# Wider rows for wo and w1, w2's last part halved, and the residual loaded by small transfers, in a decode step of grouped-query attention beside a Mish layer

## The chip, the cores and the metric

The kernel runs on one core of a Trainium2 chip. The metric is device time in microseconds, the median of three runs; every array is float32 and the batch is 8 tokens with one position each.

## What is computed

The input x (8 x 512) is normalised once, and two branches are added to it.

```python
xn = _layernorm(x, axis=-1)
return x + _A_ref(xn, A_k_cache, A_v_cache, A_wq, A_wo) + _B_ref(xn, B_w1, B_b1, B_w2)
```

Branch A is attention: q = xn @ wq gives 32 heads of 128; 8 heads of keys and values, each shared by 4 query heads, hold 8192 cached positions; p = softmax(q k / sqrt(128)), o = p v, and o @ wo (4096 x 512). Branch B is h = xn @ w1 + b1 (512 x 1792), h * tanh(softplus(h)), and then @ w2 (1792 x 512).

## The kernel before

**Memory and units.** The cached keys and values are 512 MiB of the 535 MiB that are read, and everything is read once. The work is cut into 32 units: unit j = (m, b) is the token b = j % 8 with the pair m = j // 8 of key heads. A unit has one key block k(j) and one value block v(j), each 128 rows of 64 KiB, 8 MiB (load_unit, L119). All blocks live in one large tile kv: values at V_AT, keys alternately at two places K_AT that overlap by half, w1 at W1_AT (where the second key block will come), and at the end wo over the place of the values and w2 behind it.

**One unit** (loop at L441). scores(j) multiplies the key block in two halves (L279, 64 matmuls); between the halves SP issues the next key block k(j+1) (L450). softmax(j) takes the maximum and the exponential (L289 to L313). values(j-1) multiplies the value block before (L341, 64 matmuls), after which SP issues v(j) (L458) into the place that has just come free. key_weights(j+1) (L257) prepares the next keys' weights on VectorE. turn(j) (L315) turns the exponentials for values, and merge(j-1) (L356) puts unit j-1's output, divided by the softmax sum, into oT. Once per m, at b = 4, 5, 6 and 7, load_q, project, selections and spread prepare the queries of the next pair.

**What sets the order.** The order is the program's (`tc.manual_schedule()`): each engine takes its instructions in turn, and semaphores are put in by the framework. All large transfers are issued by SP, in one queue, and an instruction of SP that waits holds all that stand behind it. x and b1 alone are issued by ScalarE.

**Start.** SP issues wq's first part (L117), k(0) (L123), w1 (L434) and k(1). w1 waits until the small region of kv that holds x and its normalised copy xc has been read. From xc TensorE makes xn4 (L185, for the queries), xnT (L187, for w1), and from x the residual xres (L193, copied at L200). Then project and spread run (L218 to L251), and the units begin.

**mish** (L362) runs in unit 0: 32 matmuls of xnT with w1, some 15 instructions on VectorE, and at last aT (L404). Its scratch lies where w1 was, so that k(2) waits for aT.

**End** (L475 to L508). wo comes in four transfers of 2 MiB (L477), w2 in four parts (L486). outputs(m) (L409) multiplies oT with wo's part m, down (L421) multiplies aT with w2's parts into H, res = H + xres (L507), and out is stored (L508).

**How the weights lie.** wo[4m:4(m+1)] is read as `u p f -> p u f`, so a partition gets four rows of 4 KiB; w1 as `j p f -> p j f`, eight rows of 3.5 KiB; w2's parts are rows of 8 KiB, the last one of 4 KiB:

```python
parts = ((0, 2), (2, 4), (4, 6), (6, 7))
for lo, hi in parts:
    t = kv[:, W2_AT + lo * BW : W2_AT + hi * BW]
    nc.sync.dma_start(t, w2_rows[:, lo * BW : hi * BW])
```

Of the kernel before, what the change touches and what calls it, by code (L numbers as in the profile page):

```python
# [14 lines left out]
B = 8  # L15
# [34 lines left out]

W2R = 7
# [10 lines left out]
LOAD_Q, MAKE_Q, SPREAD_Q = 4, 5, 7  # L62


@with_exitstack
def kernel(
# [39 lines left out]
    xnT = const.tile([P, CC, B], F32, name="xnT")  # L106
    qr = const.tile([P, DI, H2 * B], F32, name="qr")
    xres = const.tile([P, P], F32, name="xres")
    oT = const.tile([P, NP, H2, B], F32, name="oT")
# [20 lines left out]
    low = kv[:B, W1_AT : W1_AT + 3 * D]  # L130
    x_sb, xc, sq = (low[:, i * D : (i + 1) * D] for i in range(3))
# [5 lines left out]
    w1_t = kv[:, W1_AT : W1_AT + 7168].rearrange("p (j f) -> p j f", j=2 * CC)  # L137
# [5 lines left out]
    nc.gpsimd.memset(pt8, 0.0)  # L143
    for t in (H, O, M):
        nc.vector.memset(t, 0.0)
# [7 lines left out]
    nc.vector.reduce_sum(bsel, ident.rearrange("p (g q) -> p q g", g=G), axis=AX.X)  # L153
    nc.vector.reduce_sum(hsel, ident.rearrange("p (c h) -> p h c", h=H2), axis=AX.X)
# [29 lines left out]
    for c in range(CC):  # L184
        nc.tensor.transpose(M[:, c * B : (c + 1) * B], xc[:, c::CC], ident[:B, :B])  # L185
    for c in range(CC):
        nc.tensor.transpose(  # L187
            M[:, 32 + c * B : 32 + (c + 1) * B], xc[:, c * P : (c + 1) * P], ident[:B, :B]
        )
    nc.vector.tensor_copy(xn4.rearrange("p c b -> p (c b)"), M[:, 0:32])  # L190
    nc.vector.tensor_copy(xnT.rearrange("p c b -> p (c b)"), M[:, 32:64])
    for g in range(G):
        nc.tensor.matmul(  # L193
            M[Q * g : Q * g + B, 256:384],
            ident[:B, :B],
            x_sb[:, g * P : (g + 1) * P],
            start=True,
            stop=True,
        )
    nc.vector.tensor_copy(xres, M[:, 256:384])  # L200
# [12 lines left out]
    def project():  # L213

        w = ws.rearrange("p (c f) -> p c f", c=CC)
        for d in range(2):
            for c in range(CC):
                nc.tensor.matmul(  # L218
                    H[Q * c : Q * c + B, :],
                    xn4[:, c, :],  # L220
                    w[:, c, d * 512 : (d + 1) * 512],
                    start=True,
                    stop=True,
                )
            qp = work.tile([P, 512], F32, name="e")
# [12 lines left out]
        return qT  # L238
# [50 lines left out]
    def softmax(j):  # L289
# [18 lines left out]
        e = E[j] = work.tile([P, 512], F32, name="e")  # L308
# [47 lines left out]
    def merge(j, os):  # L356
        m, b = divmod(j, B)
        nc.tensor.matmul(M[:, 168 : 168 + H2], os, hsel, start=True, stop=True)  # L358
        nc.vector.tensor_mul(oT[:, m, :, b], M[:, 168 : 168 + H2], RT.pop(j))


    def mish(w1_t, b1_sb, flat):  # L362
# [5 lines left out]
        for c in range(CC):  # L368
            for g in range(G):
                nc.tensor.matmul(  # L370
                    hp[Q * g : Q * g + B, :],
                    xnT[:, c, :],
                    w1_t[:, c * 2 + g // 2, g % 2 * FG : (g % 2 + 1) * FG],
                    start=False,
                    stop=(c == CC - 1),
                )
# [32 lines left out]
    def outputs(m, t):  # L409
        w = t.rearrange("p (u f) -> p u f", u=4)  # L410
        for d in range(2):
            for h in range(REP):
                nc.tensor.matmul(
                    A[Q * h : Q * h + B, :],
                    oT[:, m, d * REP + h, :],
                    w[:, d * 2 + h // 2, h % 2 * D : (h % 2 + 1) * D],
                    start=(m == 0 and d == 0),
                    stop=(m == NP - 1 and d == 1),
                )

    def down(lo, hi, w):  # L421
        for j in range(2 * lo, 2 * hi):
            for g in range(G):
                at = (j - 2 * lo) * D + g * P
# [7 lines left out]


    nc.sync.dma_start(w1_t, w1.rearrange("j p f -> p j f"))  # L434
# [6 lines left out]
    for j in range(UNITS):  # L441
# [34 lines left out]
    for m in range(NP):  # L476
        nc.sync.dma_start(  # L477
            w_o[m].rearrange("p (u f) -> p u f", u=4),
            wo[4 * m : 4 * (m + 1)].rearrange("u p f -> p u f"),
        )  # L480
    w2_rows = w2.rearrange("j p f -> (j p) f").rearrange("(q i) f -> q (i f)", i=W2R)
    w2_t = []
    parts = ((0, 2), (2, 4), (4, 6), (6, 7))
    for lo, hi in parts:
        t = kv[:, W2_AT + lo * BW : W2_AT + hi * BW]
        nc.sync.dma_start(t, w2_rows[:, lo * BW : hi * BW])  # L486
# [7 lines left out]
    a_sb = work.tile([P, 512], F32, name="e")  # L494
# [52 lines left out]
```

## Time and profile before

| what | value |
|---|---|
| median of 3 runs | 1312.41 us (1312.4 to 1312.55) |
| the profiled execution, its own time | 1312.45 us |
| its span, first to last instruction | 1310.7 us |
| HBM read | 561.01 MB |
| PE busy | 989.0 us, 75% |
| DVE busy | 515.1 us, 39% |
| instructions | 11149 |

The span is what the profile's views cover; the 1.75 us between it and the execution's own time lie around it. Times in the views are microseconds from the span's start. PE is TensorE's matmuls, PEld its weight loads, DVE VectorE, ACT ScalarE, POOL GpSimd, SPq the queue of SyncE (SP), which issues the transfers. GB/s and the DMA share in a window are counted at the ends of packets, so that a window shorter than some microseconds swings about its mean.

### The profile page before, as it was taken

How to read it: one execution, taken by the hardware profiler on the slowest of the kernel's cores; microseconds unless marked ns; L12 is line 12 of the kernel's file. 1: busy time of each engine (PE TensorE's matmuls, PEld its weight loads, DVE VectorE, ACT ScalarE, POOL GpSimd, SP SyncE). 2: the span in 40 equal slices, each digit the busy share in tenths (PEclk: the TensorE clock that was granted, in tenths of full speed). 3: DMA queues.
4: the chain of work that ended last, by engine and by line, in shares of the span. 5: the costliest groups of instructions: out<-in, count | busy, mean ns of one | idle time of the engine just before them, and what ended most of it. 6: DMA issues, size and time to landing. Idle time of an engine off the chain costs nothing.

```text
span 1310.7 us, 11149 instructions
## 1 busy us (share of the span) xinstructions
PE 989.0 (75%) x5040; PEld 340.5 (26%) x5040; DVE 515.1 (39%) x728; ACT 40.2 (3%) x88; POOL 2.2 (0%) x9
## 2 busy tenths in 40 slices
PE   5978867768877668777878777687686678677676
PEld 3222222222322222232322222232232222222222
DVE  3364334432444442335243344414444433344421
ACT  1000000000000000000000000000000000000000
POOL 0000000000000000000000000000000000000000
PEclk9988888898888888877888888888898898888898
DMA  9999999999999999999999999999999999999997
GB/s 393 451 422 439 427 436 430 432 439 429 441 429 433 431 437 425 447 415 447 423 439 433 427 441 423 443 425 439 429 435 431 435 431 437 432 435 421 441 414 322
DMA packets 13735, 561.79 MB, mean 429 GB/s; under 512 B 1260, under 2 KB 1392, under 8 KB 4600
## 3 DMA queue, kind: packets, MB, share of 16 engines
q1 hardware_dynamic: 13664, 561.06, 99.3%
q8 instruction: 39, 0.64, 0.2%
q10 hardware_dynamic: 24, 0.02, 0.0%
q14 instruction: 8, 0.07, 0.0%
HBM read 561.01 MB, written 0.07 MB: 428 GB/s over the span
## 4 chain that ended last, share of the span: by engine, by line
DMA 72%; PE 23%; DVE 2%; SPq 2%; issue 0%; ACT 0%; DVEq 0%
DMA kv<-in_v 71%; PE o L341 20%; SPq L486 1%; DMA kv<-in_w 1%; PE s L279 1%; DVE pt L329 1%; PE x L244 1%; PE h L370 0%; PE m L229 0%; PE h L218 0%; DVE kv L392 0%; DVE tr L323 0%; DVE wk L262 0%; DVE nm L291 0%; ACT L177 0%
## 5 line engine op out<-in xcount | busy, mean ns | idle before, releaser
L279 PE MATMUL s<-kv,wk 128*64 128x512 f32 x2048 | 504.4, 655 | 174.6 <-DMA kv<-in_kT 171.9
L341 PE MATMUL o<-kv,pt 128*32 128x512 f32 x2048 | 268.6, 684 | 54.9 <-DMA kv<-in_v 45.3
L279 PEld LDWEIGHTS s<-kv,wk 128*64 128x64 f32 x2048 | 155.6, 151 | 498.0 <-issue 320.6
L329 DVE TENSOR_REDUCE pt<-tr 64x512 f32<-64x2048 f32 x64 | 241.3, 3771 | 1.6
L291 DVE TENSOR_REDUCE nm<-s 128x1 f32<-128x512 f32 x32 | 22.1, 691 | 366.7 <-PE s L279 366.7
L318 PE MATMUL x<-e,perm 128*128 128x512 f32 x256 | 128.4, 648 | 2.0 <-ACT qr L251 2.0
L341 PEld LDWEIGHTS o<-kv,pt 128*32 128x32 f32 x2048 | 69.9, 123 | 227.1 <-issue 169.6
L349 DVE TENSOR_SCALAR os<-o,isel 128x128 f32<-128x128 f32 x32 | 11.2, 351 | 274.8 <-PE o L341 274.8
L323 DVE STREAM_TRANSPOSE tr<-x 128x512 f32<-128x512 f32 x128 | 78.7, 673 | 0.0
L262 DVE TENSOR_TENSOR wk<-qr,mask 128x512 f32<-128x512 f32 x64 | 63.0, 1026 | 19.7 <-ACT qr L251 19.7
L318 PEld LDWEIGHTS x<-e,perm 128*128 128x128 f32 x256 | 50.0, 206 | 76.2 <-issue 73.7
L310 ACT ACTIVATE e<-s,nmx 128x512 f32<-128x512 f32 x32 | 22.0, 687 | 1095.7 <-DVE nmx L307 1095.7
L351 DVE SCALAR_TENSOR_TENSOR os<-o,isel,os 128x128 f32<-128x128 f32 x96 | 33.7, 351 | 3.4
L292 PE MATMUL m<-ident,nm 128*1 128x128 f32 x32 | 8.7, 273 | 29.8 <-DVE nm L291 29.8
L303 PE MATMUL m<-ident,nx 1*128 1x1 f32 x32 | 7.0, 219 | 24.1 <-DVE nx L299 24.1
L244 PE MATMUL x<-qT,tr 128*128 128x64 f32 x128 | 19.3, 315 | 3.0 <-ACT qr L251 2.7
L321 DVE RECIPROCAL rt<-m 128x8 f32<-128x8 f32 x32 | 6.6, 207 | 36.1 <-PE m L319 36.1
L244 PEld LDWEIGHTS x<-qT,tr 128*128 128x128 f32 x128 | 18.1, 226 | 6.2 <-ACT qr L251 3.3
L358 PE MATMUL m<-hsel,os 128*128 128x8 f32 x64 | 12.4, 266 | 9.3 <-DVE rt L321 9.3
L312 DVE TENSOR_SCALAR lsel<-rsel,l 128x8 f32<-128x8 f32 x32 | 7.4, 231 | 30.1 <-ACT e L310 30.1
L292 PEld LDWEIGHTS m<-ident,nm 128*1 128x1 f32 x32 | 2.5, 79 | 58.0 <-DVE nm L291 58.0
L319 PEld LDWEIGHTS m<-lsel,ones 128*128 128x128 f32 x64 | 12.2, 190 | 15.4 <-issue 15.1
(88 smaller groups left out, 163.9 us busy)
## 6 DMA issues: line engine op xcount, KB each, us to landing
ws<-in_wq SPq DMA_DIRECT2D x4, 2048.0 KB, 34.3
kv<-in_wo SPq DMA_DIRECT2D x4, 2048.0 KB, 24.3
kv<-in_w SPq DMA_DIRECT2D x1, 3584.0 KB, 26.4
kv<-in_w SPq DMA_DIRECT2D x3, 1024.0 KB, 19.3
kv<-in_kT SPq DMA_DIRECT2D x32, 29.9
kv<-in_v SPq DMA_DIRECT2D x32, 30.2
kv<-in_w SPq DMA_DIRECT2D x1, 512.0 KB, 19.5
out<-os SPq DMA_DIRECT2D x1, 64.0 KB, 1.6
```

The costliest lines, as they stand in the source:

```text
L244: nc.tensor.matmul(X[:, half, k * 64 : (k + 1) * 64], wide[:, half * 8 + k], qT, start=True, stop=True,)
L262: nc.vector.tensor_mul(w[:, :, d], q[:, :, d].to_broadcast([P, DI, NH * G, REP]), mask[:, d * NH * G : (d + 1) * NH * G] .rearrange("p (o ...
L279: nc.tensor.matmul(S[64 * c : 64 * (c + 1), :], w[:, i].rearrange("p d k h -> p (d k h)"), kk[:, i, c, :], start=(part == 0 and n == 0), s ...
L291: nc.vector.tensor_reduce(nm, S, axis=AX.X, op=ALU.max, negate=True)
L310: nc.scalar.activation(e, S, AF.Exp, bias=nmx, accum_out=l)
L318: nc.tensor.matmul(X[:, g], perm[:, g], e, start=True, stop=True)
L323: nc.vector.transpose(tr.rearrange("p (l t) c -> p t l c", t=TL)[:, tl], X.rearrange("p g (t q l) -> p t l g q", t=TL, q=PP)[:, tl],)
L329: nc.vector.tensor_reduce(pt8[half, :, :, d * REP : (d + 1) * REP].rearrange("p c y h -> p y c h"), tr[half].rearrange("p y (g c h) -> p y ...
L341: nc.tensor.matmul(O[Q * q : Q * (q + 1), :], pt8[:, c, TL * l : TL * (l + 1), :].rearrange("p t h -> p (t h)"), vt[:, 512 * n : 512 * (n ...
L351: nc.vector.scalar_tensor_tensor(os, O[:, DH * i : DH * (i + 1)], isel[:, i : i + 1], os, op0=ALU.mult, op1=ALU.add)
L358: nc.tensor.matmul(M[:, 168 : 168 + H2], os, hsel, start=True, stop=True)
L486: nc.sync.dma_start(t, w2_rows[:, lo * BW : hi * BW])
```

## The change

Five edits go together.

1. wo's parts are read as 128 rows of 16 KiB (`(p f) -> p f`), so that a partition holds eight consecutive rows of the flat part. The outputs o are turned to match: after the last token of a pair, turn_o makes oX from oT with 16 small matmuls and one copy, and outputs uses oX.
2. w1 is read as 128 rows of 28 KiB. x is turned to match: xe is xc in another order (four copies on VectorE), 8 transposes, and two masked copies (hmask, one more reduction at the start) make x8 in place of xnT.
3. w2's last part of 1024 columns becomes two of 512.
4. The residual is no longer made from x on TensorE: GpSimd clears xres, and in unit 3, behind v(3), SP issues eight transfers that bring x's rows into it.
5. The tile "e" has one buffer in place of two, and project stands behind turn and merge in place of ahead of them.

```diff
+RESIDUAL = 3
+    x8 = const.tile([P, W1R, 2, B], F32, name="x8")
+    oX = const.tile([P, NP, CC, 2, B], F32, name="oX")
...
+    xe = kv[:B, W1_AT + 3 * D : W1_AT + 3 * D + W1R * P].rearrange("b (i s) -> b i s", i=W1R)
...
+    for c in range(CC):
+        nc.vector.tensor_copy(
+            xe.rearrange("b i (c h q) -> b c i h q", c=CC, h=2)[:, c],
+            xc[:, c * P : (c + 1) * P]
+            .rearrange("b (o q i) -> b i o q", o=1, i=W1R)
+            .to_broadcast([B, W1R, 2, P // CC // 2]),
+        )
+    for i in range(W1R):
+        nc.tensor.transpose(M[:, 32 + i * B : 32 + (i + 1) * B], xe[:, i], ident[:B, :B])
+    for h in range(2):
+        nc.vector.tensor_scalar(
+            x8[:, :, h],
+            M[:, 32 : 32 + W1R * B].rearrange("p (i b) -> p i b", i=W1R),
+            hmask[:, h : h + 1],
+            None,
+            op0=ALU.mult,
+        )
...
-        nc.vector.tensor_mul(oT[:, m, :, b], M[:, 168 : 168 + H2], RT.pop(j))
+        nc.vector.tensor_mul(oT[:, :, b], M[:, 168 : 168 + H2], RT.pop(j))
+        if b == B - 1:
+            turn_o(m)
+
+    def turn_o(m):
+
+        for i in range(CC):
+            for u in range(CC):
+                nc.tensor.matmul(
+                    M[Q * u : Q * (u + 1), 256 + 2 * B * i : 256 + 2 * B * (i + 1)],
+                    ident[:, i::CC],
+                    oT[:, 2 * u : 2 * u + 2].rearrange("p h b -> p (h b)"),
+                    start=True,
+                    stop=True,
+                )
+        nc.vector.tensor_copy(
+            oX[:, m].rearrange("p i h b -> p (i h b)"), M[:, 256 : 256 + 2 * CC * B]
+        )
...
+    def residual():
+
+        for g, n in enumerate((3, 6, 7, 4)):
+            for lo, hi in ((0, n), (n, B)):
+                nc.sync.dma_start(
+                    xres[Q * g + lo : Q * g + hi, :], x[lo:hi, g * P : (g + 1) * P]
+                )
...
-    nc.sync.dma_start(w1_t, w1.rearrange("j p f -> p j f"))
+    nc.sync.dma_start(w1_t, w1.rearrange("j p f -> (j p f)").rearrange("(p i f) -> p i f", p=P, i=W1R))
...
+        if j == RESIDUAL:
+            residual()
         if more and b == LOAD_Q:
             load_q(j // B + 1)
-        if more and b == MAKE_Q:
-            qT = project()
         turn(j, lsel)
         if j > 0:
             merge(j - 1, os)
+        if more and b == MAKE_Q:
+            qT = project()
...
-        nc.sync.dma_start(
-            w_o[m].rearrange("p (u f) -> p u f", u=4),
-            wo[4 * m : 4 * (m + 1)].rearrange("u p f -> p u f"),
-        )
+        rows = wo[4 * m : 4 * (m + 1)].rearrange("u p f -> (u p f)")
+        nc.sync.dma_start(w_o[m], rows.rearrange("(p f) -> p f", p=P))
...
-    parts = ((0, 2), (2, 4), (4, 6), (6, 7))
+    parts = ((0, 4), (4, 8), (8, 12), (12, 13), (13, 14))
```

In the last line the bounds count rows of 512 columns in place of 1024, and `down` follows them; `outputs` and `mish` take the new tiles with as many matmuls as before.

More of the change, by code (lines that the diff above doesn't have):

```diff
@@ L49 @@
 NJ = PL * HALF
+W1R = 8
 W2R = 7
@@ L143 @@
     nc.gpsimd.memset(pt8, 0.0)
+    nc.gpsimd.memset(xres, 0.0)
     for t in (H, O, M):
@@ L153 @@
     nc.vector.reduce_sum(bsel, ident.rearrange("p (g q) -> p q g", g=G), axis=AX.X)
+    nc.vector.reduce_sum(
+        hmask, ident.rearrange("p (c h q) -> p h c q", c=CC, h=2), axis=AX.XY
+    )
     nc.vector.reduce_sum(hsel, ident.rearrange("p (c h) -> p h c", h=H2), axis=AX.X)
@@ L185 @@
         nc.tensor.transpose(M[:, c * B : (c + 1) * B], xc[:, c::CC], ident[:B, :B])
+    nc.vector.tensor_copy(xn4.rearrange("p c b -> p (c b)"), M[:, 0:32])
     for c in range(CC):
-        nc.tensor.transpose(
-            M[:, 32 + c * B : 32 + (c + 1) * B], xc[:, c * P : (c + 1) * P], ident[:B, :B]
-        )
[L190 to L198, printed above, removed]
+        nc.vector.tensor_copy(
[3 more added lines that the diff above has]
+            .to_broadcast([B, W1R, 2, P // CC // 2]),
+        )
+    for i in range(W1R):
[7 more added lines that the diff above has]
+            op0=ALU.mult,
         )
-    nc.vector.tensor_copy(xres, M[:, 256:384])
     wide = tr.rearrange("p y c -> p (y c)").rearrange("p (i o) -> p i o", i=DI)
@@ L224, in project @@
                 )
-            qp = work.tile([P, 512], F32, name="e")
+            qp = work.tile([P, 512], F32, name="e", bufs=1)
             nc.scalar.copy(qp, H)
@@ L307, in softmax @@
         nc.vector.tensor_copy(nmx, M[:, 128:129])
-        e = E[j] = work.tile([P, 512], F32, name="e")
+        e = E[j] = work.tile([P, 512], F32, name="e", bufs=1)
         l = work.tile([P, 1], F32, name="l")
@@ L367, in mish @@
             )
-        for c in range(CC):
+        for i in range(W1R):
             for g in range(G):
@@ L409, in outputs @@
     def outputs(m, t):
[L410 to L418, printed above, removed]
-                )
+        for n in range(2 * CC):
+            i, h = divmod(n, 2)
+            q = n % G
+            nc.tensor.matmul(
+                A[Q * q : Q * q + B, :],
+                oX[:, m, i, h],
+                t[:, n * D : (n + 1) * D],
+                start=(m == 0 and n < G),
+                stop=(m == NP - 1 and n >= 2 * CC - G),
+            )
     def down(lo, hi, w):
-        for j in range(2 * lo, 2 * hi):
+        for j in range(lo, hi):
             for g in range(G):
-                at = (j - 2 * lo) * D + g * P
+                at = (j - lo) * D + g * P
                 nc.tensor.matmul(
@@ L493 @@
     outputs(NP - 1, w_o[NP - 1])
-    a_sb = work.tile([P, 512], F32, name="e")
+    a_sb = work.tile([P, 512], F32, name="e", bufs=1)
     nc.scalar.copy(a_sb, A)
```

17 lines of the change are left out of this document (8 added, 9 removed).

## The prediction

> **What bounds the kernel now.** I read the page first, then the chain of work that ended last, then windows of the transfers, then SP's own timeline.
>
> ```profile
> span 1310.7 us, 11149 instructions
> ...
> DMA  9999999999999999999999999999999999999997
> ...
> q1 hardware_dynamic: 13664, 561.06, 99.3%
> q8 instruction: 39, 0.64, 0.2%
> ...
> DMA 72%; PE 23%; DVE 2%; SPq 2%; issue 0%; ACT 0%; DVEq 0%
> ```
>
> The page's digits show transfer engines that are busy in every slice but the last, and SP's queue (q1) fills 99.3% of them. The chain says how: the value blocks.
>
> ```profile
> 161.44 31.53 DMA kv<-in_v
> 192.97 0.04 issue
> 193.02 8.81 PE o L341 x64
> 201.83 0.02 issue
> 201.85 29.82 DMA kv<-in_v
> ```
>
> ```profile
> 100.00:1262.00 1162.00, 883.23 (x4388) 299.54 (x4388) 455.19 (x624) 30.36 (x72) 0.00 (x0) 0.87 1.00 433
> ```
>
> The last number of a window is GB/s. v(3) is issued at 161.44, lands at 192.97, is used until 201.83, and v(4) takes its place. While TensorE uses a value block, the next key block is already in the queue, so the rate stays 433 GB/s. The time is the bytes by that rate plus both ends; compute that fits beside it costs nothing, and one microsecond of empty queue costs one.
>
> The engines don't finish together, though.
>
> ```profile
> 1300.00:1304.00 4.00, 2.35 (x64) 1.43 (x60) 0.00 (x0) 0.58 (x1) 0.00 (x0) 1.00 0.56 236
> 1304.00:1307.30 3.30, 1.71 (x60) 1.13 (x53) 0.00 (x0) 0.00 (x0) 0.00 (x0) 1.00 0.37 148
> ```
>
> A share of 0.56 is 9 of 16 engines. Seven have emptied their queue by 1300, and the laggards work on until 1307: they set the end. What puts an engine behind is, I take it, the instruction loads of q8 (39 on the page), which fall on some engines and not on others.
>
> **The change, part by part.**
>
> *Rows of wo and w1.* The windows in which one kind of row moves alone:
>
> ```profile
> 29.00:35.00 6.00, 3.68 (x10) 1.21 (x12) 1.94 (x2) 0.29 (x1) 0.00 (x0) 1.00 1.03 412
> 1279.00:1290.00 11.00, 8.37 (x56) 2.15 (x60) 2.75 (x2) 0.00 (x0) 0.00 (x0) 0.66 1.02 408
> 1291.00:1298.00 7.00, 5.61 (x54) 1.37 (x46) 1.58 (x5) 0.00 (x0) 0.00 (x0) 1.00 1.03 418
> ```
>
> These are w1 (3.5 KiB rows, 412 GB/s), wo (4 KiB, 408) and w2 (8 KiB, 418). A sixteenth of 433 is 27.06 GB/s, of 408 it is 25.5: a 4 KiB row takes 160.6 ns instead of 151.4, some 9 ns over its bytes. With 9 ns a row, wo (2048 rows, 128 an engine) goes from 128 x 160.6 = 20.56 us to 32 x (605.5 + 9) = 19.66: **-0.90**. w1 goes from 64 x 139.2 = 8.91 to 8 x (1059.6 + 9) = 8.55: **-0.36**. w2's last part has 16 rows of 2 KiB an engine for 8 of 4 KiB: +0.07. Bounds, with the next item: -0.2 if long rows go no faster, -1.9 if they cost nothing over their bytes and TensorE's end shrinks to nothing.
>
> *The end.*
>
> ```profile
> 1307.23 0.04 issue
> 1307.28 0.67 PE h L425 x16
> ```
>
> Behind the last landing stand 16 matmuls, afterwards 8: **-0.3**. turn_o's last call comes ahead of it:
>
> ```profile
> 1296.65 0.17 DVE L359 TENSOR_TENSOR oT<-m,rt 128x8 f32<-128x8 f32 x1 [3.92 <-PE m L358]
> 1298.73 1.90 PE L413 MATMUL x<-kv,oT 128*8 128x512 f32 x16 [2.12 <-DMA kv<-in_wo]
> 1300.74 0.58 ACT L495 COPY e<-x 128x512 f32<-128x512 f32 x1 [42.86 <-PE x L413]
> 1301.60 1.06 PE L425 MATMUL h<-kv,aT 128*8 128x128 f32 x32
> 1303.57 1.06 PE L425 MATMUL h<-kv,aT 128*8 128x128 f32 x32 [0.91 <-DMA kv<-in_w]
> 1306.04 1.06 PE L425 MATMUL h<-kv,aT 128*8 128x128 f32 x32 [1.42 <-DMA kv<-in_w]
> ```
>
> TensorE waits 2.1 us for wo here and 0.9 + 1.4 us for w2. wo and w2 come about 1.2 us earlier afterwards, so some 3.2 us for turn_o are covered. Its 16 products cost 16 x 66 ns = 1.1 us by the small matmuls of L425 (32 instructions are 16 products) and 16 x 0.39 = 6.2 us by L358 below, whose weights are four times wider. I take 2, nearer to L425, plus a copy of 0.2: hidden, nothing. The three earlier calls stand in a gap:
>
> ```profile
> 165.44 0.39 PE L358 MATMUL m<-hsel,os 128*128 128x8 f32 x2 [0.30 <-DVE rt L321]
> ...
> 173.66 15.72 PE L279 MATMUL s<-kv,wk 128*64 128x512 f32 x64 [7.84 <-DMA kv<-in_kT]
> ```
>
> TensorE waits 7.84 us for the key block behind merge. project in its new place uses the same gap; its work is the same, and the single "e" is read out before its next writer in both orders.
>
> *The start.* w1's issue waits for four copies on VectorE and 8 transposes more, about 2 us by the rows of L183 (0.47 us for 512 elements) and L187 (0.57 for 4); project comes that much later.
>
> ```profile
> 8.87 0.47 DVE L183 TENSOR_SCALAR kv<-kv,st 8x512 f32<-8x512 f32 x1
> 9.96 0.57 PE L187 MATMUL m<-ident,kv 8*128 8x8 f32 x4
> ...
> 11.63 0.38 SPq L434 DMA_DIRECT2D kv<-in_w  x1
> 48.27 0.33 SPq L123 DMA_DIRECT2D kv<-in_v  x1
> 67.75 0.33 SPq L123 DMA_DIRECT2D kv<-in_kT  x1
> ```
>
> Ahead of w1 are 10.5 MB, 24 us of transfers from 1.7 us on; ahead of v(0) at 48.27 they last until about 55; ahead of k(2) at 67.75 until about 74. The cover is over 5 us each time, so 2 us cost nothing.
>
> *The eight transfers.* Their 16 KB are nothing. But each transfer signals a semaphore, and the trace's records of SP's transfers name it:
>
> ```
> 89.61 v(1) 100 | 106.31 k(3) 102 | 124.45 v(2) 103 | 144.43 k(4) 104 | 161.44 v(3) 107
> 182.56 k(5) 108 | 201.85 v(4) 109 | 202.23 wq 110 | 222.38 k(6) 100
> ```
>
> Eight semaphores go round. The same records show SP waiting for a semaphore's earlier transfer before it is given out again: ahead of k(3) it waits for 102, which wq's first part had signalled and which k(3) has no other reason to wait for. Eight transfers behind v(3) take one full turn: the seventh gets k(4)'s semaphore, and the **eighth gets that of v(3) itself**. So SP stands in front of the eighth until v(3) has landed, and k(5) stands behind it.
>
> ```profile
> 182.56 0.33 SPq L123 DMA_DIRECT2D kv<-in_kT  x1
> ```
>
> k(5) is issued at 182.56 now, 10.4 us before v(3) lands at 192.97. With the wait it comes at 192.97 + 0.33 for the eighth + 0.1 = 193.4, and nothing else is queued: all 16 engines run dry, once. How long does a restart take?
>
> ```profile
> 0.74 0.37 SPq L117 DMA_DIRECT2D ws<-in_wq  x1
> ```
>
> ```profile
> 0.00:1.70 1.70, 0.00 (x0) 0.00 (x0) 0.72 (x2) 0.06 (x1) 1.10 (x8) 1.00 0.02 4
> 1.70:27.20 25.50, 14.94 (x75) 10.60 (x75) 7.79 (x32) 5.19 (x8) 1.10 (x2) 1.00 0.99 415
> ```
>
> ```profile
> out<-os SPq DMA_DIRECT2D x1, 64.0 KB, 1.6
> ```
>
> 25.5 us at 415 GB/s are 10.58 MB, 24.4 us at 433: the stream counts as begun at 2.8, 2.0 us after the issue. A store's last bytes land 1.6 us after its issue. I take 2.0, from the nearer row, and get 195.4. When did the engines end v(3)?
>
> ```profile
> 190.00:191.00 1.00, 0.27 (x1) 0.08 (x1) 0.60 (x5) 0.00 (x0) 0.00 (x0) 1.00 1.37 590
> 191.00:192.00 1.00, 0.22 (x1) 0.13 (x1) 0.30 (x3) 0.29 (x1) 0.00 (x0) 1.00 0.46 197
> 192.00:193.00 1.00, 0.00 (x0) 0.00 (x0) 0.23 (x1) 0.48 (x2) 0.00 (x0) 1.00 0.76 328
> ```
>
> 590, 197 and 328 GB/s in one microsecond are 9, 3 and 5 packets of 65.5 KB, one an engine each 2.42 us: most engines end v(3) near 190.8, the late ones near 192.5. Counted from the late ones, the hole is 195.4 - 192.5 = **+2.9** (from 1.9, if the stream is full 0.96 us after the issue, where the window of 4 GB/s ends, to 3.2, if the eighth's issue takes twice 0.33 us; the store's 1.6 us lie between).
>
> Besides, all 16 start level again. An engine that was early at 190.8 loses its lead of 1.7 us. Whether that reaches the end depends on who is last there: if the instruction loads go round, an engine not yet hit by 193 has as many hits ahead of it as any, and is among the last. If the last one at the end is one that was late already, nothing is lost. Between 0 and 1.7 I take **+1.4**: the last two windows hold 8 packets, so at least one of the 9 engines that are late at 1300 was early at 193.
>
> *Sum.* -0.90 - 0.36 + 0.07 - 0.3 = -1.5 for rows and end; +2.9 + 1.4 = +4.3 for the eighth transfer; together **+2.8 us**. The profiled execution took 1312.45 us, its span 1310.7; the 1.75 us around it don't change, and its time is the median's 1312.41 within 0.04. So 1315.2. The ends: -1.9 + 1.9 + 0 = 0 (1312.4) and -0.2 + 3.2 + 1.7 = +4.7 (1317.1).
>
> The Trainium skill, "DMA: Bandwidth & Descriptors", section "Specifications", gives about 0.6 us to the first byte on the path that SP uses; the window above has almost nothing within 0.96 us of the issue, so the trace speaks against it here. By it alone the restart would be an estimated 1.4 us shorter and the sum 1313.8.
>
> **The rivals.**
>
> *The eighth doesn't wait* (not slower than before). If the framework deals out semaphores otherwise when transfers are as small as these, or has a ninth, k(5) is issued at 182.56 as now and the queue never empties. It decides at one point: whether the eighth's semaphore is v(3)'s. Then only rows and end are left: 1312.4 - 1.5 = 1310.9. The full turn of eight in the records above speaks against it; that no wait of this kind costs anything in the trace of before leaves room. 0.09.
>
> *Small transfers hold the engines.* If each of the eight has the store's 1.6 us to itself in the queue, that is 12.8 us on top of -1.5: 1323.7. Against it: blocks issued one behind another leave no hole, 433 GB/s over 1162 us. The Trainium skill, same page, section "Rules for kernel authors", says that transfers under 64 KB pay mostly overhead and should be coalesced; by that rule this rival would be the outcome, and by the rows the overhead is hidden behind what is queued. 0.03.
>
> *turn_o becomes the bound at the end.* At 0.39 us a product it takes 6.2 us, 3 more than the waits cover, and TensorE ends after the transfers: 1315.2 + 3 = 1318.2. L425's 66 ns speaks against it. 0.04.
>
> *The start starves.* If the copies into xe cost over 2 us each and not 0.5, v(0) and k(2) are issued after the queue has emptied; every microsecond over the cover of 5 costs one. At 8 us late it would be 1315.2 + 3 = 1318.2 too. 0.02.
>
> **How the numbers follow.** The forecast, the stall at the eighth transfer, has the remaining 0.82: 1315.2, and nearly all of that case between 1313.0 and 1316.8. That is the range; it leaves out the 0.09 below and the 0.09 above. 0.2% is 2.6 us, about what a measurement of this kernel can tell from no change, so the forecast lies just beyond the bound at 1315.03, and the case is split by it: 0.46 above and 0.36 below, since the hole and the lead could each be a microsecond smaller. Slower has 0.46 and the three rivals above it, 0.09: 0.55. Of the 0.09 without a stall 0.02 go to faster, for which rows and end would have to give nearly twice their sum, and 0.07 to within 0.2%: 0.43.
>
> **What would show it.** In the profile afterwards: SP's timeline has the eighth small transfer at about 192.7, as v(3) lands, and k(5) behind it at about 193.1 in place of 182.56; a window there falls far under 433 GB/s, and k(5) lands some 2 us later than now. The windows of w1 and wo show about 427 GB/s or more in place of 412 and 408. The waits for w2 stay the last ones of the chain, with 8 matmuls behind the last. I am wrong if k(5) is still issued 10 us ahead of v(3)'s landing; if TensorE's turn_o stands in the chain of work that ended last; or if the queue has a hole in the first 100 us.

## The result and the profile after

The kernel after takes 1317.11 us (median of 6 runs, 1315.02 to 1318.97), the kernel before beside it 1312.47 us (1312.4 to 1313.25). The ratio is 1.0034, with a 95% interval of 1.0021 to 1.0047: slower, by 4.6 us. The forecast was 1315.2 with a range to 1316.8. The sign and the main cause were right; the median lies 0.3 us above the range, and the experiments show why. The profiled execution took 1316.18 us, 0.9 less than the median.

The page of the kernel after:

```profile
span 1314.4 us, 11489 instructions
...
DMA  9999989999999999999999999999999999999998
...
q1 hardware_dynamic: 11440, 561.08, 99.0%
q8 instruction: 40, 0.66, 0.2%
...
DMA 57%; PE 34%; DVE 8%; issue 1%; ACT 1%; SPq 0%; ACTq 0%; DVEq 0%
```

One digit of the transfer engines has fallen to 8 inside the span: the sixth slice, which is 164 to 197 us. In the chain TensorE has 34% in place of 23, VectorE 8 in place of 2. SP's timeline shows what happens in that slice.

```profile
163.45 0.33 SPq L128 DMA_DIRECT2D kv<-in_v  x1
163.83 30.14 SPq L469 DMA_DIRECT2D xres<-in_x  x8
194.06 0.36 SPq L128 DMA_DIRECT2D kv<-in_kT  x1
202.18 0.35 SPq L128 DMA_DIRECT2D kv<-in_v  x1
```

The eight small transfers take SP 30.14 us, and k(5) is issued behind them, at 194.06 where it was 182.56. SP's waits say for what it stood (us in total, times, longest):

```profile
SPq L469 <- DMA kv<-in_v: 19.1, 1, 19.1
...
SPq L469 <- DMA kv<-in_kT: 8.6, 1, 8.6
```

That is 8.6 us for a key block, k(4), in front of the seventh, and 19.1 us for a value block, v(3), in front of the eighth, in the order that the round of semaphores gives. The windows around it (the last three columns are granted clock, DMA share and GB/s; the second view looks more closely behind k(5)'s issue):

```profile
182.00:190.00 8.00, 8.00 (x40) 2.67 (x38) 0.00 (x0) 0.00 (x0) 0.00 (x0) 1.00 0.96 418
190.00:191.00 1.00, 0.78 (x4) 0.00 (x0) 0.17 (x1) 0.00 (x0) 0.00 (x0) 1.00 0.36 142
191.00:192.00 1.00, 0.27 (x1) 0.08 (x1) 0.64 (x2) 0.00 (x0) 0.00 (x0) 1.00 0.01 2
192.00:193.00 1.00, 0.22 (x1) 0.13 (x1) 0.65 (x5) 0.00 (x0) 0.00 (x0) 0.99 0.00 0
193.00:194.00 1.00, 0.25 (x4) 0.20 (x8) 0.09 (x2) 0.78 (x2) 0.00 (x0) 0.50 0.01 1
194.00:195.00 1.00, 1.00 (x8) 0.20 (x4) 0.15 (x1) 0.00 (x0) 0.00 (x0) 0.50 0.01 2
195.00:196.00 1.00, 1.00 (x8) 0.20 (x4) 0.00 (x0) 0.00 (x0) 0.00 (x0) 0.50 2.72 934
```

```profile
194.06:195.03 0.97, 0.97 (x8) 0.20 (x4) 0.09 (x1) 0.00 (x0) 0.00 (x0) 0.50 0.01 2
195.03:195.13 0.10, 0.10 (x4) 0.00 (x0) 0.00 (x0) 0.00 (x0) 0.00 (x0) 0.50 8.00 2621
```

From 191 to 195 next to nothing is counted. To read this, a sentence ahead of the prediction has to be put right: a packet is counted whole in the window in which it starts, not at its end. The 934 GB/s from 195 to 196 are 14 packets of 65.5 KB, four of them in a tenth of a microsecond, and such a packet takes an engine 2.42 us by the prediction's own reading; none that was issued at 194.06 could have ended by 196. So the last packets of v(3) start before 191 and are through by 193.4, and the next ones start from 195.03 on: even the engine that ended last stands idle for 1.6 us or more, and by the records of the packets those that ended first for over 4. The first packets are slower, too: a share of 2.72 of 16 engines in one microsecond is 3.1 us for each of the 14.

The wider rows show as well, w1 in the first window below, wo in the second:

```profile
29.00:35.00 6.00, 3.36 (x11) 1.62 (x12) 1.93 (x2) 0.58 (x1) 0.00 (x0) 1.00 1.03 444
1283.00:1294.00 11.00, 9.90 (x72) 2.57 (x76) 1.69 (x4) 0.00 (x0) 0.00 (x0) 0.74 1.01 426
```

They were 412 and 408 GB/s. The end of TensorE's timeline, and the end of the chain:

```profile
1299.91 0.67 PE L382 MATMUL m<-oT,ident 128*32 128x16 f32 x32 [0.27 <-DVE oT L374]
...
1302.42 3.52 PE L445 MATMUL x<-kv,oX 128*8 128x512 f32 x16 [1.83 <-DMA kv<-in_wo]
...
1309.86 1.68 PE L457 MATMUL h<-kv,aT 128*8 128x128 f32 x48 [1.01 <-DMA kv<-in_w]
```

```profile
1271.46 38.35 DMA kv<-in_w
1309.86 1.73 PE h L457 x48
1311.66 0.29 DVE os L547
```

turn_o's last call takes 0.67 us and TensorE still waits 1.83 us for wo behind it. The chain ends with w2, and 48 matmul instructions stand behind the landing that counts.

One thing in the text ahead of the prediction is wrong, and has to be put right here: it says that mish takes its new tiles with as many matmuls as before. It has twice as many. With 28 KiB rows a partition holds eight consecutive rows of the flat w1, each x8 slice is half masked, and 8 x 4 products take the place of 4 x 4. In the timelines of before and of after:

```profile
51.10 4.79 PE L370 MATMUL h<-kv,xnT 128*8 128x448 f32 x32
```

```profile
51.08 6.20 PE L402 MATMUL h<-kv,x 128*8 128x448 f32 x64
```

### The profile page after: what moved, and what is told of

The parts are those of the page before. It is cut to its first block, busy times and chain, and to the rows that moved or that the text cites. A ratio compares the mean times of both kernels' runs of the same rounds, so it can differ in the third digit from the quotient of the medians.

```text
span 1314.4 us, 11489 instructions
## 1 busy us (share of the span) xinstructions
PE 990.2 (75%) x5196; PEld 343.7 (26%) x5196; DVE 517.6 (39%) x737; ACT 40.2 (3%) x88; POOL 2.3 (0%) x10
## 4 chain that ended last, share of the span: by engine, by line
DMA 57%; PE 34%; DVE 8%; issue 1%; ACT 1%; SPq 0%; ACTq 0%; DVEq 0%
DMA kv<-in_v 54%; PE o L356 20%; PE s L294 9%; DVE pt L344 4%; DMA kv<-in_w 3%; PE x L333 2%; DVE tr L338 1%; PE m L244 1%; PE h L233 1%; PE x L259 1%; PE h L402 0%; DVE nm L306 0%; ACT e L241 0%; DVE kv L424 0%; DVE nr L311 0%
## 5 line engine op out<-in xcount | busy, mean ns | idle before, releaser
L333 PE MATMUL x<-e,perm 128*128 128x512 f32 x256 | 120.1, 612 | 2.0 <-ACT qr L266 2.0
L277 DVE TENSOR_TENSOR wk<-qr,mask 128x512 f32<-128x512 f32 x64 | 62.9, 1024 | 19.8 <-ACT qr L266 19.8
L333 PEld LDWEIGHTS x<-e,perm 128*128 128x128 f32 x256 | 46.6, 192 | 73.6 <-issue 71.2
L244 PE MATMUL m<-bsel,e 128*128 128x8 f32 x64 | 14.9, 362 | 30.4 <-DVE oT L374 26.7
L244 PEld LDWEIGHTS m<-bsel,e 128*128 128x128 f32 x64 | 14.2, 327 | 42.0 <-issue 29.4
L382 PE MATMUL m<-oT,ident 128*32 128x16 f32 x128 | 2.7, 219 | 29.6 <-DVE oT L374 29.6
```

Of the source, the lines that this page charges most:

```text
L244: nc.tensor.matmul(M[:, at : at + B], qp[:, h * DH : (h + 1) * DH], bsel[:, :B], start=True, stop=True,)
L277: nc.vector.tensor_mul(w[:, :, d], q[:, :, d].to_broadcast([P, DI, NH * G, REP]), mask[:, d * NH * G : (d + 1) * NH * G] .rearrange("p (o ...
L333: nc.tensor.matmul(X[:, g], perm[:, g], e, start=True, stop=True)
```

## The experiments

Theories. **The wait**: the eighth transfer carries v(3)'s semaphore, SP stands until v(3) has landed, and that costs over 4 us. **The start**: w1's part makes the first units late; v(1) is issued when the queue has run empty. **The place**: project and turn_o, now behind merge, wait for VectorE's long reductions and hold TensorE back. In the expectations S is the wait ("stall") in the first four runs and the start in the last four; E is the start as well, and P the place. A ratio is against the kernel before, run beside it on the same chip, whose median was between 1312.47 and 1312.57 us in every comparison; a difference in us is against that median. The runs with v(1) late spread over some us, so medians that differ by less than a microsecond between two such kernels decide nothing.

### How many small transfers

The kernel after with six, or seven, transfers in place of eight, the same rows in all:

```diff
-        for g, n in enumerate((3, 6, 7, 4)):
-            for lo, hi in ((0, n), (n, B)):
+        for g, cuts in enumerate(((3,), (6,), (), ())):      # seven: ((3,), (6,), (7,), ())
+            for lo, hi in zip((0, *cuts), (*cuts, B)):
```

> After with six residual transfers in place of eight (the last two column groups in one transfer of 8 rows each); nothing else. Theory S (stall): semaphores go round in eight, so the one of v(3) is now given to the second transfer behind k(5), not to one ahead of it. k(5) is issued near 183 us again, not 194, the windows from 190 to 196 keep 433 GB/s, and the time falls by the hole and the lost lead, some 4 us: 1312.5 to 1313.5. Theory P (late TensorE): project and turn_o now stand behind VectorE's long reductions (project's second step waits 8.9 us three times), and late issues of k and v are what costs; then the time stays at 1316 or more and its spread over the runs stays some 4 us wide.

> After with seven residual transfers (only the last column group in one). Theory S: the eighth transfer behind v(3) is now k(5) itself, so k(5) carries v(3)'s semaphore and is issued only when v(3) has landed, near 193.5 us: the hole stays and the time is that of after within 1 us (1316 to 1318). If it is the small transfers themselves that cost, by their number, seven lie one quarter of the way from eight to... four of eight: some 0.5 us below after. Theory P: as after, 1317.

Six: 1313.36 us (1311.23 to 1314.88, 11 runs), ratio 1.0004 (0.9995 to 1.0012). SP's timeline:

```profile
94.12 0.33 SPq L128 DMA_DIRECT2D kv<-in_v  x1
...
163.37 2.04 SPq L469 DMA_DIRECT2D xres<-in_x  x6
184.00 0.36 SPq L128 DMA_DIRECT2D kv<-in_kT  x1
```

Six transfers take SP 2.04 us, k(5) is back at 184.00, and the window from 190 to 196 shows 451 GB/s. The two transfers fewer are worth 3.8 us. Seven: 1316.54 us (1315.55 to 1318.34, 5 runs), ratio 1.0031 (1.0019 to 1.0043).

```profile
165.19 10.47 SPq L469 DMA_DIRECT2D xres<-in_x  x7
194.79 0.36 SPq L128 DMA_DIRECT2D kv<-in_kT  x1
```

With seven, the small transfers end at 175.7 (SP has waited 8.3 us of that for k(4)), and it is k(5) itself that carries v(3)'s semaphore and waits for its landing. So the count decides, not the eighth row of x: seven or eight transfers between v(3) and the next block that must not be late bring a full turn of the eight semaphores.

The same transfers alone, in the kernel before:

```diff
-    for g in range(G):
-        nc.tensor.matmul(M[Q * g : Q * g + B, 256:384], ident[:B, :B], x_sb[...], ...)
-    nc.vector.tensor_copy(xres, M[:, 256:384])
+    nc.gpsimd.memset(xres, 0.0)
...
+        if j == RESIDUAL:
+            residual()
```

> Before with the residual by eight transfers in unit 3, and no other part of the change (the 8 matmuls and the copy that made the residual from x are gone). Theory S: k(5) is issued near 193 us, the queue has a hole of 2 to 3 us, and the time is 1312.5 + 4.3 = 1316.8. Theory P: 1312.5 to 1313, since project and turn_o aren't touched.

1316.75 us (1316.32 to 1316.9, 6 runs), ratio 1.0031 (1.002 to 1.0042).

```profile
163.63 29.72 SPq L430 DMA_DIRECT2D xres<-in_x  x8
193.45 0.36 SPq L124 DMA_DIRECT2D kv<-in_kT  x1
```

The wait alone costs 4.2 us, with a spread of only 0.6 (without the residual's matmuls w1 is issued 1 us earlier there, at 10.67). What spreads the runs of after over 4 us is another part.

### The place of project and turn_o

In after, project's second step waits for VectorE; its timeline in unit 5, both engines:

```profile
251.62 7.56 DVE L344 TENSOR_REDUCE pt<-tr 64x512 f32<-64x2048 f32 x2
259.21 0.17 DVE L374 TENSOR_TENSOR oT<-m,rt 128x8 f32<-128x8 f32 x1
259.53 1.85 PE L244 MATMUL m<-bsel,e 128*128 128x8 f32 x8 [8.90 <-DVE oT L374]
```

TensorE stands 8.90 us for merge's product into oT, which VectorE does behind 7.56 us of turn's reductions. Before, project stood ahead of turn and did not see them. The edit puts project back and turn_o one unit later (and gives project another buffer, so that "e" stays single):

```diff
-        if b == B - 1:
+        if j == UNITS - 1:
             turn_o(m)
...
+            if j > B and b == 1:
+                turn_o(j // B - 1)
...
+        if more and b == MAKE_Q:
+            qT = project()
         turn(j, lsel)
         if j > 0:
             merge(j - 1, os)
-        if more and b == MAKE_Q:
-            qT = project()
```

> After with project ahead of turn again (its copy of H goes into the part of the query weights that has just been read, so that no second buffer is needed) and turn_o, but for the last, one unit later behind values, where nothing waits for VectorE; the eight transfers stay. Theory S: the stall stays, 1316 to 1317; TensorE's late starts go, but they cost next to nothing, so the median falls by less than 1 us. Theory P: 1313 or less, and the runs agree within 0.3 us as they do before.

> Both earlier edits together: six residual transfers, project ahead of turn, turn_o one unit later. No stall at v(3) remains in it. Rows and end were worth 1.5 us by the prediction, so 1311.0 if nothing else costs. Six transfers alone gave 1313.36 with runs from 1311.2 to 1314.9, and its trace shows the queue running short near 94, 590 and 1023 us. Theory P (late TensorE behind project and turn_o, the holes at 590 and 1023): both go, 1311 to 1312, spread under 1 us. Theory E (early: mish has 64 matmul instructions in place of 32 and begins 1.3 us later, so v(1) is issued up to 94 us, when the queue runs dry): the hole near 94 stays, 1312.3 to 1313.3, with runs that differ by 2 us.

> Before with one buffer of e and project behind turn and merge, nothing else. Theory P: its second step waits some 9 us for VectorE in units 5, 13 and 21, the key blocks behind are issued later, and the queue runs short after some of them: 1313 to 1314, with runs that differ. If the slack covers it: 1312.57 and as narrow as before.

After with this edit: 1316.93 us (1315.29 to 1317.3, 6 runs), ratio 1.0031 (1.0019 to 1.0043), 0.2 less than after. With six transfers as well: 1311.69 (1311.06 to 1313.1, 11 runs), 0.9993 (0.9984 to 1.0001), 1.7 less than six alone. The kernel before with project behind merge and one buffer "e": 1312.51 (1312.33 to 1313.84, 11 runs), 1.0000 (0.9991 to 1.0008). Three answers, 0.2, 1.7 and 0: a wait of 8.9 us that costs nothing in the kernel before cannot be the cause by itself. Moved back one at a time, with six transfers:

> The kernel after with six residual transfers and project ahead of turn again; turn_o and the start stay. Theory S (the start: v(1) is issued when the queue empties, near 94 us, and that alone makes the time and its spread): as with six transfers alone, 1313.4, over 2 us of spread. Theory P (project behind merge holds TensorE back and the time with it): 1311.7, as when project and turn_o were both moved.

> The kernel after with six residual transfers and turn_o one unit later; project stays behind merge. Theory S: 1313.4 with over 2 us of spread. Theory P, if turn_o is its cause and not project: 1311.7; if project is: 1313.4.

project alone: 1312.27 us (1311.0 to 1314.54, 11 runs), 1.0000 (0.9991 to 1.0009). turn_o alone: 1311.99 us (1311.02 to 1313.82, 11 runs), 0.9997 (0.9989 to 1.0006). Neither value that the theories gave came: both spread over the whole width of six alone, and both lose something. By themselves these two decide nothing. Nor does the place alone explain the 1.7 us between six and six with both moved, since the same wait of project cost the kernel before nothing; the next runs look at the start.

### w1's part and the start

Here w1 goes back to `j p f -> p j f` with xnT and 16 products, in the kernel of six and place, and in the kernel after; and w1's part alone goes into the kernel before.

```diff
-    nc.sync.dma_start(w1_t, w1.rearrange("j p f -> (j p f)").rearrange("(p i f) -> p i f", p=P, i=W1R))
+    nc.sync.dma_start(w1_t, w1.rearrange("j p f -> p j f"))
...
-        for i in range(W1R):
+        for c in range(CC):
...
-                    x8[:, i, g // 2],
+                    xnT[:, c, :],
```

> As e5, with w1 back in eight rows of 3.5 KiB, xnT and mish as before; wo's rows, turn_o, w2's halved part and six residual transfers stay. Theory E: the start is as early as before, v(1) is issued at 87 to 90 us and the hole near 94 goes; 1312.57 - 0.9 (wo) - 0.3 (end) = 1311.4, with a spread as before's, 0.5 us. Theory P: no gain over e5, but the 0.36 us of w1's rows lost.

> After with w1 back in eight rows of 3.5 KiB, xnT and mish as before; the eight residual transfers, project and turn_o stay where the change puts them. If w1's part costs what it cost by itself (0.7 us in the median, up to 3.8): 1316.2 to 1316.6 and a narrower spread than 1315.0 to 1319.0, since the queue doesn't run short near 94 us. If the stall and project alone make the spread, the time and the spread are those of after.

> Before with w1 in rows of 28 KiB, x8 and the longer mish, and nothing else of the change (one buffer of e, and project's copy of H in the query weights that have been read, to make room). Theory E: v(1) is issued 2 to 4 us later than now (89.6), the queue runs short near 94 us, and the loss eats the rows' 0.36 us or more: 1312.5 to 1314, runs 1 to 2 us apart. If the start doesn't matter: 1312.2, runs within 0.5 us.

With the old w1 beside six and place: 1311.70 us (1311.57 to 1311.92, 11 runs), 0.9993 (0.9984 to 1.0002); the same median as with the new one, but 0.4 us of spread in place of 2. In the kernel after: 1315.97 (1315.66 to 1316.57, 8 runs), 1.0027 (1.0016 to 1.0037); 1.1 less than after, and 0.9 us of spread in place of 4. w1's part alone in the kernel before: 1313.19 (1312.04 to 1316.3, 11 runs), 1.0008 (0.9999 to 1.0017), 0.7 more where 0.36 less was forecast. The interval takes in 1, but the runs spread over 4.3 us, as those of after do; the profiled execution took 1315.42 us. SP's timeline and the window of 94 to 95 us there:

```profile
95.39 0.33 SPq L125 DMA_DIRECT2D kv<-in_v  x1
```

```profile
94.00:95.00 1.00, 1.00 (x16) 0.12 (x4) 0.00 (x0) 0.00 (x0) 0.00 (x0) 1.00 0.00 0
```

No packet starts in that microsecond, and v(1) is issued after it, when the queue has run empty. Is it the longer mish, or the later start? The kernel before with 16 more products of zero weights in mish, which add nothing to the sum, and nothing else:

```diff
+                nc.tensor.matmul(hp[Q * g : Q * g + B, :], zero, w1_t[...], start=False, stop=False)
```

> Before with mish's 16 products done twice, the first time with weights of zero, which add nothing to the result; the start ahead of it is as before and w1 lies as before. If the doubled mish is what makes v(1) late: v(1) is issued 1.5 to 3 us later than 89.6, the queue runs short near 94, and the runs spread to 1313 to 1315, the median 1312.7 to 1313.3. If the later start of project is needed for it too: 1312.5 to 1312.6, as before.

1312.60 us (1312.39 to 1314.24, 11 runs), 1.0003 (0.9994 to 1.0012): hardly anything, and v(1) is issued at 89.58 in its profiled execution, as before. So the other half is tried: the kernels with six and with eight transfers, project and turn_o left as in after, with the start alone shortened. x is spread out in qr, which is free then, and not in the region that w1 is loaded into, and its eight transposes stand inside project's waits:

```diff
-    xe = kv[:B, W1_AT + 3 * D : W1_AT + 3 * D + W1R * P].rearrange("b (i s) -> b i s", i=W1R)
+    xe = qr[:B].rearrange("b i c -> b (i c)").rearrange("b (i s) -> b i s", i=W1R)
...
             nc.scalar.copy(qp, H)
+            if first:
+                for i in range(W1R // 2 * d, W1R // 2 * (d + 1)):
+                    nc.tensor.transpose(M[:, 32 + i * B : 32 + (i + 1) * B], xe[:, i], ident[:B, :B])
```

> The kernel after with six residual transfers, and the start shortened: x is spread out in qr and no longer in the region that w1 is loaded into, and its eight transposes stand inside project's waits. project and turn_o stay as in the kernel after. Theory S: v(1) issued below 92.5 in place of 94.12, most runs between 1311.0 and 1311.9. Theory P: 1313.0 or more, since project and turn_o are untouched.

> The kernel after with the start shortened in the same way; eight transfers, project and turn_o stay. Theory S: most of the 1.14 us that w1's part costs in the kernel after goes, 1316.0 or a little less, in place of 1317.1. Theory P, or if the longer mish costs and not its late start: 1317.1.

Six: 1311.17 us (1310.94 to 1315.76, 11 runs, nine of them to 1311.8), 0.9996 (0.9987 to 1.0005). Eight: 1315.40 us (1314.94 to 1317.28, 11 runs), 1.0024 (1.0016 to 1.0033). The shorter start takes 2.2 us off the one and 1.7 off the other, with project and turn_o where the change put them. So it is the start. The 1.7 is less sure than the 2.2: after has six runs, and they overlap with those of its short start. With the short start, moving project and turn_o as well leaves the median where it is (1311.18, below), so that a few tenths at most are left for the place. The rate from 27 to 100 us, with six transfers, then with six and the short start:

```profile
27.00:100.00 73.00, 62.68 (x313) 21.63 (x314) 33.36 (x52) 4.00 (x7) 0.00 (x0) 0.93 1.00 423
```

```profile
27.00:100.00 73.00, 60.75 (x309) 19.97 (x310) 38.14 (x54) 4.00 (x7) 0.00 (x0) 0.91 1.01 436
```

423 in place of 436 GB/s over 73 us are 73 x 13 / 436 = 2.2 us. And that is nearly all of it: at 100 us six has moved 1.0 MB less (415 and 425 GB/s from 0 on), and at 1300 us it has 1.1 MB more to move (162 and 89 GB/s over the 15 us that follow), 2.3 and 2.5 us at 433 GB/s. So in these two executions project's waits cost next to nothing. The profiled executions side by side, from the windows and timelines of each:

| kernel | granted clock 49 to 60 us | mish, us | v(1) issued | GB/s 27 to 100 us | this execution, us |
|---|---|---|---|---|---|
| before | 0.84 | 4.79 | 89.61 | 437 | 1312.45 |
| six, short start | 1.00 | 6.20 | 89.31 | 436 | 1310.94 |
| six, project moved | 1.00 | 6.20 | 91.08 | 434 | 1311.95 |
| six, turn_o moved | 0.84 | 7.52 | 93.77 | 422 | 1312.95 |
| six | 0.84 | 7.80 | 94.12 | 423 | 1313.69 |
| six, both moved | 1.00 | 6.20 | 91.46 | 431 | 1313.10 |
| six, both moved, short start | 0.69 | 9.06 | 92.15 | 434 | 1313.60 |
| after, short start | 1.00 | 6.20 | 87.90 | 437 | 1315.49 |
| after | 1.00 | 6.20 | 91.28 | 435 | 1316.18 |
| after, both moved | 1.00 | 6.20 | 90.11 | 435 | 1315.29 |
| seven | 0.69 | 8.94 | 94.18 | 422 | 1317.32 |
| before, w1's part | 0.69 | 9.02 | 95.39 | 421 | 1315.42 |

With v(1) up to about 92 the stretch has lost 1 us at most; at 93.8 and later it has lost over 2. And the new mish is not equally long in each execution: 6.20, 7.5 to 7.8 or about 9.0 us, with the granted clock at 1.00, 0.84 or 0.69. The windows of after and of six:

```profile
49.00:60.00 11.00, 10.20 (x81) 3.34 (x82) 4.81 (x12) 2.64 (x4) 0.00 (x0) 1.00 1.09 471
```

```profile
49.00:60.00 11.00, 9.45 (x78) 2.07 (x74) 3.57 (x9) 2.06 (x3) 0.00 (x0) 0.84 1.07 465
```

The Trainium skill, "TensorE: Matmul & The Clock Gate", section "Part 1: The HAM clock gate (the "warmup" mystery)", says that TensorE runs at half its clock until a free-running window of about 3.4 us has been busy, so that the cold time differs from run to run. One such window at half clock in 11 us would be an estimated mean of 1 - 0.5 x 3.4 / 11 = 0.85, two of them 0.69: the three values of the trace agree. In seven the granted clock is 0.51 from 51.00 to 57.70 us and 1.00 in the 1.9 us before. So a good part of the spread of the kernels with a late start is, I argue, this clock: a cold mish costs nothing while v(1) has some us in hand, and up to 3 us when it has none. Only profiled executions show their clock, so that this holds for each single run is not shown. And it is not the whole spread: six with both moved had the full clock and yet took 1313.10 us, 2.2 more than six with the short start, of which the stretch to 100 us explains 0.8.

### wo's part, and a better kernel

The kernel before with wo's rows, oX and turn_o (one unit later), and nothing else but project's buffer:

```diff
-            w_o[m].rearrange("p (u f) -> p u f", u=4),
-            wo[4 * m : 4 * (m + 1)].rearrange("u p f -> p u f"),
+        rows = wo[4 * m : 4 * (m + 1)].rearrange("u p f -> (u p f)")
+        nc.sync.dma_start(w_o[m], rows.rearrange("(p f) -> p f", p=P))
```

> Before with wo in rows of 16 KiB, oX and turn_o (one unit later, behind values), w1, w2 and the residual untouched (one buffer of e, project's copy of H in the read query weights). The prediction's term for wo is -0.9: 1311.6, as narrow as before. If turn_o's last call is the bound at the end, no gain: 1312.5.

1311.67 us (1311.55 to 1312.07, 11 runs), 0.9994 (0.9985 to 1.0002): 0.87 less, every run below the lowest run of before (1312.2). Its window of wo:

```profile
1279.00:1290.00 11.00, 8.35 (x58) 2.15 (x61) 2.77 (x2) 0.00 (x0) 0.00 (x0) 0.67 1.01 429
```

All that helped together: six transfers, the place, and the short start.

> e5 (both rows, six transfers, project and turn_o placed, w2 halved) with the start's extra work out of the way: xe lies where w1 doesn't come, and its 8 transposes stand where TensorE waits for ScalarE in project. v(0) is issued 1 us earlier than in e5, which leaves the longer mish alone. If that is enough: 1311.0 to 1311.3 and runs within 0.5 us, under both e6 and before. If the longer mish suffices for the hole near 94 us, 1311.5 to 1312 with runs 1 to 2 us apart.

1311.18 us (1310.99 to 1313.6, 11 runs), 0.9993 (0.9984 to 1.0001). Eight of the 11 runs lie between 1310.99 and 1311.26. Its profiled execution was the longest, 1313.6. Its mish was cold (clock 0.69, 9.06 us), but with the short start v(1) still came at 92.15, and from 27 to 100 us it has 434 GB/s: what it lost is not in the start. The windows of the end, of six with the short start (1310.94 us) and of this one:

```profile
1300.00:1315.00 15.00, 4.02 (x120) 2.87 (x120) 0.29 (x1) 0.19 (x1) 0.00 (x0) 0.98 0.23 89
```

```profile
1300.00:1315.00 15.00, 5.91 (x136) 3.20 (x136) 0.29 (x1) 0.59 (x1) 0.00 (x0) 0.94 0.29 116
```

At 1300 us it has 15 x 27 GB/s, or 0.41 MB, more to move, 0.9 us at 433 GB/s. The other 1.7 of the 2.7 us are lost behind 1300 us, where the transfer engines run out of work one after another; why they end less evenly here is open. So a short start doesn't end the spread: six with it has one run of 1315.76, too. The median is 1.4 us below that of before, and the same as with the short start and six transfers alone (1311.17); the interval just takes in 1.

## Why the prediction was right in the cause and too low in the time

**The eighth transfer: right in its cause, its place and its total; the two parts of the total were not, and that they add up is in part luck.** Forecast +4.3 us, measured +4.2 alone in the kernel before and 1315.40 - 1311.17 = 4.2 between eight and six with the short start. The rival that the eighth does not wait is refuted by the 19.1 us that SP stands for v(3). k(5) was forecast at 193.4 (193.1 among the signs) and came at 194.06; v(3) landed at 193.70 in place of 192.97. As to the parts, the prediction took 2.0 us from the issue to the stream, and the first packets start 1.0 us after it. That is 0.6 us after the end of the issuing instruction (194.42 and 195.03), as in its own rows of the start (1.11 and 1.70), so that the trace does not speak against the 0.6 us that it set aside. And it took the windows before for ends of packets: its 190.8 and 192.5 are starts, some of them k(5)'s. So the hole behind the last engine is under 2 us in place of 2.9. The rest is the lead that the earlier engines lose, and slower first packets, which the prediction did not have. By the records of the packets an engine stands idle for 3.1 us on average in the kernel before with eight transfers (4.0 in after), and its first packet then takes some 0.7 us longer: 3.8 of the 4.2. The rival of small transfers that hold the engines falls with six of them: they cost SP 2.04 us, and with the short start that kernel is 1.3 us below the kernel before.

**wo's rows: right.** Forecast -0.90, measured -0.87. **w1's rows: right in kind, too small.** Forecast -0.36; with the short start, eight transfers and the new w1 stand 2.93 us over their kernel before, and with the old w1 3.43: -0.5. With six transfers and both moved it is the same: -1.36 with the new w1 and the short start, -0.83 with the old w1.

**The start: this is the step that failed.** It read "The cover is over 5 us each time, so 2 us cost nothing". The working looked at v(0) and k(2) alone. The next issue in the quoted rows of the semaphores is v(1) at 89.61, and it was not checked: by the table it had between 2 and 4 us in hand. And the delay was too small. The 2 us for copies and transposes were about right: w1 is issued at 14.07 for 11.63 with w1's part alone, at 12.90 in after, where the residual's matmuls have left the start. But I had taken mish for unchanged, and at the full clock it has 6.20 us in place of 3.19 (the 32 instructions on xnT in the kernel with zero weights): 3.0 us more, so 4.3 together. In six v(1) is 4.5 us later than in before; in the profiled executions of before and after only 1.7 of it show, since before's mish ran at a clock of 0.84. k(2) follows the end of mish by 11.9 us in before (55.89 and 67.75) and in after (57.28 and 69.13), and v(1) follows k(2) by 21.9 and 22.2 there, so every microsecond arrives. What it cost in the kernel after is 1317.11 - 1315.40 = **1.7 us** by the medians; the one profiled execution of after, with v(1) at 91.28, shows little of it. The sign that the prediction named for this, a hole in the first 100 us, came in six, in seven and with w1's part alone (421 to 423 GB/s from 27 to 100 us, against 437 in before). The rival "the start starves" had this outcome, at the wrong blocks and with copies of over 2 us as its condition; it got 0.02, because its condition left mish out. The longer mish alone (the kernel with zero weights) stays within the margin, and so does the new mish behind the short start; the two together don't. With the start repaired the kernel after takes 1315.40 us, and the forecast was 1315.2.

**project's place: wrong as written, without a price that can be shown.** "project in its new place uses the same gap" is wrong: it waits 8.90 us in a gap that it had not seen. That raised TensorE's and VectorE's share of the chain; with the short start and project left in place the shares stay (33% and 8%), but no time is left over for them. Summed against before: +4.2 - 0.87 - 0.5 = 2.8, and the kernel after with the short start stands 2.9 over it. The remaining 0.1 holds the end, project and turn_o together.

**The end: mis-sized.** Forecast -0.3, with 8 matmuls behind the last landing. In after 48 stand there, 1.68 us: the third part of w2 is what lands last in the chain, and the 32 matmuls of it with the 16 of the halves keep TensorE busy for longer than the halves take to come (0.52 MB at 433 GB/s, 1.2 us). Before, 1.2 us of transfer and 0.67 stood there; so the gain is 1.87 - 1.73 = 0.1, worked out and not measured by itself. **turn_o hidden at the end: right**, at 0.67 us where 2 were taken, and the rival that it sets the end falls with the 1.83 us that TensorE still waits.

**Open:** the price of project's and turn_o's waits one by one, which the spread of the late start hides (from 1016 to 1026 us six has 369 GB/s and six with project moved 374, but 454 with turn_o moved and 433 with the short start; whether that reaches the end is not shown); why six with both moved is 1.7 us below six, whose start is the same; what makes the engines end less evenly in some executions; and that the granted clock, run by run, makes the rest of the spread.

## What to carry to other kernels

Count the transfers between one big block and the next that must not be late: where completion semaphores go round, a full turn of small transfers makes the queue wait for the block itself, and that, not their bytes, is the price. When a start is made later, follow the delay to every later issue of the queue, not only to the first ones, and count the instructions of each stage again after a change of layout; the cover that one block has is no cover for the next. And where a stage's margin is as small as the clock's own variation, the median may move by which runs happened to be cold: repair the margin first, then compare the rest.

## What the runs showed that was not expected

The granted clock of one short stage had three levels, 1.00, 0.84 and 0.69, in executions of nearly the same program, and the stage 6.20, 7.8 and 9.0 us. In the kernel before, with its margin, this doesn't reach the time: its profiled execution had 0.84 there, too, and 437 GB/s from 27 to 100 us. Its window:

```profile
49.00:60.00 11.00, 10.22 (x54) 3.29 (x56) 6.12 (x15) 2.64 (x4) 0.00 (x0) 0.84 0.93 400
```

And a wait of 8.90 us on TensorE (project's, in the kernel before with project behind merge too) cost nothing that eleven runs could show, while 4 us of delay ahead of v(1) cost 2: not the length of the wait counts, but what the queue holds behind it.
